# One head's exponential in every eighth forward unit moved from ScalarE to VectorE, its value product eight units later

## The chip, the cores and the metric

The kernel runs on one core of a Trainium2 chip (trn2). The metric is the device time of one execution in microseconds; the median of the runs is compared. The engines are TensorE (PE, with its weight loads as PEld), VectorE (DVE), ScalarE (ACT), GpSimd (POOL) and SyncE (SP, which only issues DMAs here).

## The reference, cut to what matters

One transformer block with adaptive layer norm, forward, and then the gradients of everything by its inputs and weights. One sequence of 2048 tokens, width 512, 32 heads of 16, a dense part of width 1792 with a squared ReLU. The change touches the attention of the forward pass only:

```python
h = _layernorm(x, axis=-1) * (1 + ca) + sa
qkv = (h @ wqkv).reshape(B, S, 3, H, Dh)          # H = 32, Dh = 16
scores = jnp.einsum('bhqd,bhkd->bhqk', q, k) * Dh ** (-0.5)
p = softmax(scores, axis=-1)
o = jnp.einsum('bhqk,bhkd->bhqd', p, v)
x = x + ga * (o.reshape(B, S, D) @ wo)            # then the dense part, then jax.vjp of it all
```

The softmax needs 32 x 2048 x 2048 exponentials in the forward pass; the backward pass computes them once more.

## The kernel before, in words

The program runs in four stages on one core: a short preparation, the forward pass with its attention (up to 996 us), the last quarter of the dense part, and then the attention's backward pass (from about 1100 us) with the gradients of the projections at the end. The instruction order of all engines is the order of the Python code (a manual schedule): each engine takes its own instructions strictly in that order.

**Forward units.** The attention is cut into 512 units: 4 query chunks of 512 tokens (`qc`), 8 head groups of 4 heads (`hg`), 16 key tiles of 128 tokens (`kt`, the innermost loop). In the loop over `u`, `fscore(u)` issues four score products on TensorE (L576: keys x queries, 128 x 512 per head). They go into two PSUM tiles `psST` of two banks each, one for each pair of heads; the pool holds three such tiles. ScalarE turns each tile into bfloat16 exponentials with one 128x1024 instruction (L578), into the unit's SBUF tile `ET`, of which there are four. Two units later `fpv(u)` multiplies the four heads' exponentials with the values (L592), in four 32-column strips of the array, and adds them into the one PSUM bank `oacc`. After the sixteenth key tile VectorE copies `oacc` out (`ostage`, L596); a row of ones in the values gives the softmax's denominator with it. The maximum is bounded beforehand and enters through an extra row of the queries, so that no maximum is taken over the scores. Two idle products of `steady` (L615) fill units that have no other product.

**Work fitted between.** The unit loop also carries everything else of the forward pass. A plan of tasks by unit number fills the first 100 units: the other heads' projections, norms, transposes. From unit 130 on, `dense_chunk` runs as a generator, one product per unit, over the dense part of the query chunk just finished (chunks 0, 1 and 2; the fourth comes after the forward units). Its parts are, in order: the attention output and its layer norm (L348 to L377), the first dense product with ReLU and square (L410, L412, L413), the dense gradient (L424, L427), four long sums each for the input gradient (L446) and the dense output (L500), and the attention gradient (L532). Between them `next_chain` issues weight gradients (L233) and VectorE copies each out (`part`, L251). All these products share a single PSUM bank (`mm()`, tag `pm`, a pool of one): a product can't begin before VectorE has emptied the bank of the one before it.

**Order on the engines.** A unit issues, in this order: what `later(lag, ...)` has put off to this unit (`run_due`), the scores and exponentials of unit u, the value products of unit u-2, the planned task or the dense step with its evictions. VectorE does the evictions and all elementwise work of the dense part; GpSimd sums rows (`racc`, L170), scales (`gf_c`, L307), copies `obf` (L604) and issues the loads of keys and queries.

Of the kernel before, what the change touches and what calls it, by code (L numbers as in the profile page):

```python
# [28 lines left out]
SCALE = 0.25  # L29
EPS = 1e-5  # L30
QPAD = 528


@with_exitstack
def kernel(
# [111 lines left out]
    with ExitStack() as ph:  # L147
# [32 lines left out]
        def later(lag, f, *args):  # L180
            due.append((unit[0] + lag, f, args))
# [371 lines left out]

        funits = [(qc, hg, kt) for qc in range(QC) for hg in range(HG) for kt in range(TT)]
        fh, fe, fcur, fdone, dense = {}, {}, {}, [], []

        def fload(qc, hg):
            i = hg % 2
# [8 lines left out]
        def fscore(u):  # L567
            qc, hg, kt = funits[u]
            qt_sb, kt_sb = fh[qc, hg]
            ET = ework.tile([P, 4, 512], BF, name="ET", tag="ET")  # L570
            fe[u] = ET
            for pair in range(2):
                ps = pools["s"].tile([P, 2, 512], F32, name="psST", tag="psST")
                for hi in range(2):
                    r = 32 * (2 * pair + hi)
                    PE.matmul(ps[:, hi, :], kt_sb[r:r + 32, kt * P:(kt + 1) * P], qt_sb[r:r + 32, :],  # L576
                              start=True, stop=True, tile_position=(r, 0))
                ACT.activation(ET[:, 2 * pair:2 * pair + 2, :], ps[:], AF.Exp, scale=SCALE)  # L578

        def fpv(u):  # L580
            qc, hg, kt = funits[u]
            if kt == 0:
                fcur["o"] = pools["o"].tile([P, 512], F32, name="oacc", tag="oacc")
                if hg == 0:
                    fcur["rr"] = ework.tile([H, 512], F32, name="rrows", tag="rrows", bufs=1)
                    fcur["ou"] = ework.tile([P, 4, HG, P], BF, name="O_un", tag="O_un", bufs=1)
            oacc = fcur["o"]
            ET = fe.pop(u)
            for hq in range(4):
                h = hg * 4 + hq  # L590
                lhsT = vaug[:, kt].rearrange("p h c -> p (h c)")[:, h * (DH + 1):h * (DH + 1) + 32]
                PE.matmul(oacc[32 * hq:32 * hq + 32, :], lhsT, ET[:, hq, :],  # L592
                          start=(kt == 0), stop=(kt == TT - 1), tile_position=(0, 32 * hq), skip_group_check=True)
            if kt == TT - 1:
                ostage = ework.tile([P, 512], F32, name="ostage", tag="ostage", bufs=1)
                DVE.tensor_copy(ostage[:], oacc[:])  # L596
                obf = ework.tile([P, 512], BF, name="obf", tag="obf", bufs=2)
                if u == NF - 1:
                    fcur["last"] = ostage
                    return  # L600
                if hg == HG - 1:
                    DVE.tensor_copy(obf[:], ostage[:])
                else:
                    POOL.tensor_copy(obf[:], ostage[:])  # L604
                for hq in range(4):
                    h = hg * 4 + hq
                    later(2, sp, fcur["rr"][h:h + 1, :], ostage[32 * hq + 16:32 * hq + 17, :])
                later(3, sp, fcur["ou"][:, :, hg, :], obf[:], True)
                if hg == HG - 1:
                    fdone.append((u + 7, qc, fcur["rr"], fcur["ou"]))  # L610
# [622 lines left out]
        def last_chunk(O_c, L, w1T, w2T):  # L1233
# [29 lines left out]
            for half in range(2):  # L1263
# [30 lines left out]
                for ic in range(DC):  # L1294
# [4 lines left out]
                    else:  # L1299
                        DVE.tensor_scalar(to, pt[:, :, ic, :], modcol[:, 4, ic:ic + 1], modcol[:, 3, ic:ic + 1],  # L1300
                                          ALU.mult, ALU.add)
            db2bf = wk.tile([1, D], BF, name="db2bf", tag="db2", bufs=1)
            later(4, DVE.tensor_tensor, db2bf[:], pd[0:1, :], gb_bc[0:1, :], ALU.mult)
            later(6, sp, out_7.rearrange("(o f) -> o f", o=1), db2bf[:])
            later(len(dwq) + 2, sp, h2_c.rearrange("p t (i d) -> p (t i) d", d=P), h2T.rearrange("p t i q -> p (t i q)"), True)
# [716 lines left out]
```

## Time and profile before

| what | value |
|---|---|
| time, median of 3 runs | 2491.31 us (2484.18, 2491.31, 2497.56) |
| profiled execution, span from first to last instruction | 2501.3 us; the page gives no other time of that execution |
| mean granted TensorE clock | 0.980 |
| busy over the span: PE, ACT, DVE, POOL | 2324.0, 2303.7, 1837.7, 488.0 us |
| forward units: first and last start of an exponential | 41.2 and 995.1 us |
| exponentials L578 | 1024 instructions, 941.9 us busy |
| backward exponentials L1600 | 2048 instructions of 128x512 |

A group line gives the code line, the engine, the operation, what it writes and reads with shapes, the count, the busy time and the mean duration of one, and then the engine's idle time just before. Durations of neighbouring instructions of one engine overlap somewhat, so the rate of a group is read from the distance of starts or ends, not from the mean duration.

### The profile page before, as it was taken

How to read it: one execution, taken by the hardware profiler on the slowest of the kernel's cores; microseconds unless marked ns; L12 is line 12 of the kernel's file. 1: busy time of each engine (PE TensorE's matmuls, PEld its weight loads, DVE VectorE, ACT ScalarE, POOL GpSimd, SP SyncE). 2: the span in 40 equal slices, each digit the busy share in tenths (PEclk: the TensorE clock that was granted, in tenths of full speed). 3: DMA queues.
4: the chain of work that ended last, by engine and by line, in shares of the span. 5: the costliest groups of instructions: out<-in, count | busy, mean ns of one | idle time of the engine just before them, and what ended most of it. 6: DMA issues, size and time to landing. Idle time of an engine off the chain costs nothing.

```text
span 2501.3 us, 49888 instructions
## 1 busy us (share of the span) xinstructions
PE 2324.0 (93%) x18948; PEld 783.4 (31%) x19036; DVE 1837.7 (73%) x2377; ACT 2303.7 (92%) x3560; POOL 488.0 (20%) x661
## 2 busy tenths in 40 slices
PE   8899899989998998999999999999999999999989
PEld 3232233223332333443223323233232323332344
DVE  6555354455435444579989999999999999999965
ACT  7999999999998999539999999999999999999944
POOL 2111223323533453110111101111011110110100
PEclk9999999999998999999999999999999999999999
DMA  4468463258546865979999999999999999999984
GB/s 146 130 167 176 144 150 97 88 166 142 98 95 142 151 131 110 256 200 196 201 192 206 199 198 202 196 204 203 205 205 198 205 202 199 200 198 214 201 253 133
DMA packets 1189503, 437.70 MB, mean 175 GB/s; under 512 B 1065867, under 2 KB 1160521, under 8 KB 1188878
## 3 DMA queue, kind: packets, MB, share of 16 engines
q1 hardware_dynamic: 1152414, 389.35, 79.0%
q0 software_dynamic: 19872, 27.09, 6.5%
q10 hardware_dynamic: 16976, 18.07, 2.9%
q8 instruction: 149, 2.44, 0.4%
q14 instruction: 92, 0.75, 0.1%
HBM read 98.30 MB, written 70.80 MB: 68 GB/s over the span
## 4 chain that ended last, share of the span: by engine, by line
ACT 40%; PE 38%; issue 8%; DVE 7%; DMA 3%; SPq 1%; ACTq 1%; POOL 0%; DVEq 0%; another core or an unknown queue 0%; POOLq 0%
ACT E_u L1600 24%; ACT ET L578 12%; PE dqacc L1681 4%; PE psST L576 3%; PE psS_A L1594 3%; PE accVK L1654 2%; PE pm L233 2%; ACT dsT L1760 2%; PE psS_B L1594 2%; PE pdh L1858 2%; PE oacc L592 2%; PE psS_C L1594 2%; PE pwq L1892 2%; PE pm L500 2%; PE pm L410 2%
## 5 line engine op out<-in xcount | busy, mean ns | idle before, releaser
L1616 DVE TENSOR_TENSOR dS_u<-psD_u,E_u 128x1024 bf16<-128x1024 f32 x1024 | 1185.9, 1218 | 77.1 <-PE psD_u L1614 30.2
L578 ACT ACTIVATE ET<-psST 128x1024 bf16<-128x1024 f32 x1024 | 941.9, 1242 | 16.6 <-PE psST L576 16.3
L1600 ACT ACTIVATE E_u<-psS_A 128x512 bf16<-128x512 f32 x768 | 509.9, 664 | 10.8 <-PE psS_C L1594 8.5
L1600 ACT ACTIVATE E_u<-psS_B 128x512 bf16<-128x512 f32 x768 | 503.2, 655 | 10.8 <-DMA dsT<-dS_u 2.7
L1614 PE MATMUL psD_u<-iv,ido 32*128 32x512 bf16 x2048 | 409.1, 388 | 1.5 <-DVE dS_u L1616 1.3
L576 PE MATMUL psST<-qt_sb,kt_sb 32*128 32x512 bf16 x2048 | 313.8, 386 | 48.0 <-ACT ET L578 41.0
L1600 ACT ACTIVATE E_u<-psS_C 128x512 bf16<-128x512 f32 x512 | 334.3, 653 | 3.1 <-PE psS_B L1594 1.1
L1594 PE MATMUL psS_B<-ik,iq 32*128 32x512 bf16 x768 | 296.1, 386 | 11.7 <-ACT E_u L1600 4.4
L1594 PE MATMUL psS_A<-ik,iq 32*128 32x512 bf16 x768 | 294.5, 383 | 11.0 <-DVE dwlast L237 1.0
L1699 POOL TENSOR_TENSOR dQacc<-dQacc,dqtmp 128x512 f32<-128x512 f32 x64 | 81.2, 1268 | 858.8 <-ACT dqtmp L1694 797.4
L1594 PEld LDWEIGHTS <-iq 32*128 32x128 bf16 x2048 | 129.7, 91 | 313.9 <-issue 296.9
L1654 PE MATMUL accVK<-dS_u,qz 128*32 128x512 bf16 x2048 | 213.5, 388 | 0.5 <-PE psD_u L1614 0.2
L592 PE MATMUL oacc<-ET,vaug 128*32 128x512 bf16 x2048 | 207.0, 394 | 3.9 <-DVE ostage L596 3.9
L1663 PE MATMUL accVK<-E_u,dOs_tok 128*16 128x512 bf16 x2048 | 204.5, 388 | 0.0
L1594 PE MATMUL psS_C<-ik,iq 32*128 32x512 bf16 x512 | 194.2, 379 | 4.5
L576 PEld LDWEIGHTS <-kt_sb 32*128 32x128 bf16 x2048 | 84.3, 91 | 328.2 <-issue 306.5
L1681 PE MATMUL dqacc<-dsT,KS_tok 128*32 128x512 bf16 x2048 | 145.7, 382 | 18.8 <-DMA dsT<-dS_u 5.0
L1760 ACT ACTIVATE dsT<-ptT 128x1024 bf16<-128x1024 bf16 x128 | 144.1, 1126 | 13.1 <-PE ptT L1644 12.2
L251 DVE COPY part<-pm 128x512 f32<-128x512 f32 (+2 forms) x106 | 65.2, 615 | 121.9 <-PE pm L233 111.8
L1614 PEld LDWEIGHTS <-ido 32*128 32x128 bf16 x2048 | 105.2, 91 | 101.3 <-issue 94.9
L1654 PEld LDWEIGHTS <-qz 128*32 128x32 bf16 x2048 | 58.5, 94 | 178.0 <-issue 162.9
L1699 POOL TENSOR_TENSOR dQst<-dQacc,dqtmp 128x512 bf16<-128x512 f32 x32 | 40.6, 1270 | 266.1 <-ACT dqtmp L1694 266.1
(415 smaller groups left out, 2688.7 us busy)
## 6 DMA issues: line engine op xcount, KB each, us to landing
p_st<-part POOLq DMA_DIRECT2D x36, 256.0 KB, 4.6
kt_sb<-qkT_st POOLq DMA_DIRECT2D x124, 64.0 KB, 3.0
wA<-in_B_w_dram SPq DMA_DIRECT2D x28, 256.0 KB
wB<-w1T_st SPq DMA_DIRECT2D x21, 256.0 KB
wA<-w2T_st SPq DMA_DIRECT2D x21, 256.0 KB
wB<-in_B_w_dram SPq DMA_DIRECT2D x21, 256.0 KB
p_st<-part POOLq DMA_DIRECT2D x28, 192.0 KB, 4.6
p_st<-part SPq DMA_DIRECT2D x18, 256.0 KB
```

Source lines behind the costliest of these rows:

```text
L576: PE.matmul(ps[:, hi, :], kt_sb[r:r + 32, kt * P:(kt + 1) * P], qt_sb[r:r + 32, :], start=True, stop=True, tile_position=(r, 0))
L578: ACT.activation(ET[:, 2 * pair:2 * pair + 2, :], ps[:], AF.Exp, scale=SCALE)
L592: PE.matmul(oacc[32 * hq:32 * hq + 32, :], lhsT, ET[:, hq, :], start=(kt == 0), stop=(kt == TT - 1), tile_position=(0, 32 * hq), skip_grou ...
L1594: PE.matmul(psS[:], st["q"][r:r + 32, qt * P:(qt + 1) * P], st["k"][r:r + 32, kc * 512:kc * 512 + 512], start=True, stop=True, tile_positi ...
L1600: ACT.activation(bst[u][0][:, hq, :], sst.pop((u, hq))[:], AF.Exp, scale=SCALE)
L1614: PE.matmul(psD[:, hi, :], st["do"][r:r + 32, qt * P:(qt + 1) * P], st["v"][r:r + 32, kc * 512:kc * 512 + 512], start=True, stop=True, til ...
L1616: DVE.tensor_tensor(dS_u[:, 2 * pair:2 * pair + 2, :], psD[:], E_u[:, 2 * pair:2 * pair + 2, :], ALU.mult)
L1654: PE.matmul(cur["vk"][32 * hq:32 * hq + 32, :], hst[hg]["qz"][:, qt, hq, :], bst[u][1][:, hq, :], start=(qt == 0), stop=False, tile_positi ...
L1663: PE.matmul(acc[32 * hq:32 * hq + DH, :], dOs_tok[:, qt, (hg * 4 + hq) * DH:(hg * 4 + hq + 1) * DH], E_u[:, hq, :], start=False, stop=(qt ...
L1681: PE.matmul(acc[32 * hq:32 * hq + 32, :], KS_tok[:, kc * 4 + kt, h * DH:h * DH + 32], tT[:, :, hq * 4 + kt, :], start=(kt == 0), stop=(kt ...
L1699: POOL.tensor_tensor(dst2, dst, tmp[:], ALU.add)
L1760: ACT.activation(dst, pt[:], AF.Identity)
```

## The change

In the units with `kt % 8 == 1` (64 of 512, two in each run of sixteen) the second pair's instruction on ScalarE covers only the third head (128x512). The fourth head goes to `vector_exp`: VectorE reads the score bank, multiplies by `SCALE*log2(e)` and clips, splits the exponent into an integer and a fraction by adding and subtracting a rounding constant, shifts the integer into the exponent bits, evaluates a polynomial of degree 4 of the fraction, and multiplies both into a bfloat16 result. These are nine instructions over 128x512, all but the last result in fp32: the first at once, the others one per unit over the next seven units, two of them in the third. The value product of that head is issued eight units after its scores, ahead of the four (or three) products of that moment, into the same `oacc`. It lies in the same head group: key tile 1's is issued with key tile 7, key tile 9's with key tile 15.

Three fp32 scratch tiles of 128x512 are added in SBUF; `ET` has three buffers instead of four, `obf` one instead of two, and a small tile of the last dense chunk takes its space from another ring.

```diff
+LOG2E = 1.4426950408889634
+ROUND = 12583039.0
+POW2 = (-0.6931241750717163, 0.24024099111557007, -0.055906426161527634, 0.009582852944731712)
...
-            ET = ework.tile([P, 4, 512], BF, name="ET", tag="ET")
+            ET = ework.tile([P, 4, 512], BF, name="ET", tag="ET", bufs=3)
...
-                ACT.activation(ET[:, 2 * pair:2 * pair + 2, :], ps[:], AF.Exp, scale=SCALE)
+                if pair == 1 and kt % 8 == 1:
+                    ACT.activation(ET[:, 2, :], ps[:, 0, :], AF.Exp, scale=SCALE)
+                    vector_exp(u, ps[:, 1, :])
+                else:
+                    ACT.activation(ET[:, 2 * pair:2 * pair + 2, :], ps[:], AF.Exp, scale=SCALE)
+
+        def vector_exp(u, s):
+            w, t, p = (ework.tile([P, 512], F32, name=f"vx{i}", tag=f"vx{i}", bufs=1) for i in range(3))
+            bits, res = t[:].bitcast(I32), p[:].bitcast(BF)[:, 0:512]
+            DVE.tensor_scalar(w[:], s, SCALE * LOG2E, -126.0, ALU.mult, ALU.max)
+            later(1, DVE.tensor_scalar, t[:], w[:], ROUND, None, ALU.add)
+            later(2, lambda: DVE.scalar_tensor_tensor(out=w[:], in0=t[:], scalar=ROUND, in1=w[:], op0=ALU.subtract, op1=ALU.subtract))
+            later(3, DVE.tensor_scalar, bits, bits, 23, None, ALU.logical_shift_left)
+            later(3, DVE.tensor_scalar, p[:], w[:], POW2[3], None, ALU.mult)
+            for lag, i, to in ((4, 2, p), (5, 1, p), (6, 0, w)):
+                later(lag, lambda i=i, to=to: DVE.scalar_tensor_tensor(out=to[:], in0=p[:], scalar=POW2[i], in1=w[:], op0=ALU.add, op1=ALU.mult))
+            later(7, lambda: DVE.scalar_tensor_tensor(out=res, in0=w[:], scalar=1.0, in1=t[:], op0=ALU.add, op1=ALU.mult))
+            flate[u + 8] = (u, res)
+
+        def value_product(u, hq, src):
+            h = funits[u][1] * 4 + hq
+            kt = funits[u][2]
+            lhsT = vaug[:, kt].rearrange("p h c -> p (h c)")[:, h * (DH + 1):h * (DH + 1) + 32]
+            PE.matmul(fcur["o"][32 * hq:32 * hq + 32, :], lhsT, src,
+                      start=(kt == 0), stop=(kt == TT - 1), tile_position=(0, 32 * hq), skip_group_check=True)
...
             ET = fe.pop(u)
+            if u + 2 in flate:
+                value_product(flate[u + 2][0], 3, flate.pop(u + 2)[1])
             for hq in range(4):
-                h = hg * 4 + hq
-                lhsT = vaug[:, kt].rearrange("p h c -> p (h c)")[:, h * (DH + 1):h * (DH + 1) + 32]
-                PE.matmul(oacc[32 * hq:32 * hq + 32, :], lhsT, ET[:, hq, :],
-                          start=(kt == 0), stop=(kt == TT - 1), tile_position=(0, 32 * hq), skip_group_check=True)
+                if hq < 3 or kt % 8 != 1:
+                    value_product(u, hq, ET[:, hq, :])
...
-                obf = ework.tile([P, 512], BF, name="obf", tag="obf", bufs=2)
+                obf = ework.tile([P, 512], BF, name="obf", tag="obf", bufs=1)
...
-            db2bf = wk.tile([1, D], BF, name="db2bf", tag="db2", bufs=1)
+            db2bf = wk.tile([P, D], BF, name="db2bf", tag="dxn2")[0:1, :]
```

More of the change, by code (lines that the diff above doesn't have):

```diff
@@ L555 @@
         fh, fe, fcur, fdone, dense = {}, {}, {}, [], []
+        flate = {}
         def fload(qc, hg):
```

## The prediction

> **What bounds the kernel now.** I read the page's slices first, then the exponentials' tile view, the windows by stage, and at last the timeline of single units.
>
> ```profile
> PE   8899899989998998999999999999999999999989
> DVE  6555354455435444579989999999999999999965
> ACT  7999999999998999539999999999999999999944
> ```
>
> The forward units fill the first sixteen slices. ScalarE is full there; VectorE is half free.
>
> ```profile
> L578 ACT ACTIVATE ET<-psST x1024: 1018/1206/1959, 41.2 to 995.1; 128x1024 bf16<-128x1024 f32 x171
>   PE psST L576: 16.3, 16
> ```
>
> From the first start to the last are 953.9 us, of which ScalarE waited 16.3. The rest is (953.9 - 16.3)/1023 = 0.917 us an exponential, 1.83 a unit. So the forward is ScalarE's, and time taken from ScalarE there counts if nothing else is nearly as slow. TensorE waits for ScalarE only in places; the next two views show what stands close behind.
>
> ```profile
> 566.65 0.57 PE L576 MATMUL psST<-qt_sb,kt_sb 32*128 32x512 bf16 x4
> 566.76 0.75 DVE L412 TENSOR_SCALAR rT<-pm,b1col 128x512 bf16<-128x512 f32 x1 [0.66 <-PE pm L410]
> 567.15 0.40 PE L592 MATMUL oacc<-ET,vaug 128*32 128x512 bf16 x4
> 567.55 0.42 DVE L413 TENSOR_TENSOR sT<-rT 128x512 bf16<-128x512 bf16 x1
> 567.57 1.02 PE L410 MATMUL pm<-h2T,wA 128*128 128x512 bf16 x4
> 568.52 0.53 PE L576 MATMUL psST<-qt_sb,kt_sb 32*128 32x512 bf16 x4
> ```
>
> This is one unit of the first dense product. The product starts 0.06 after the eviction before it ends (566.76 + 0.75), runs 1.02, and 0.04 to 0.1 later VectorE evicts again: a loop over the single bank, 568.52 - 566.65 = 1.87 us a unit, already longer than ScalarE's 1.83. A lead that TensorE brings along (three score tiles: 2 x 0.917 less about 0.5 for release and scores, 1.3 us) hides the difference over 14 units. VectorE has 0.66 free in each such unit.
>
> ```profile
> core 0: us, PE busy (x) PEld busy (x) DVE busy (x) ACT busy (x) POOL busy (x), PEclk, DMA share, GB/s
> 41.00:996.25 955.25, 860.24 (x5994) 283.25 (x6056) 473.11 (x933) 941.94 (x1024) 312.45 (x490) 0.99 0.58 132
> 187.00:201.00 14.00, 13.54 (x105) 4.45 (x102) 11.92 (x28) 14.00 (x17) 5.22 (x10) 1.00 0.58 121
> 331.00:345.00 14.00, 13.04 (x93) 4.77 (x93) 10.94 (x16) 14.00 (x17) 6.33 (x9) 1.00 0.51 125
> 604.00:643.00 39.00, 35.07 (x252) 12.41 (x256) 15.40 (x34) 39.00 (x43) 18.12 (x35) 1.00 0.91 125
> 780.00:799.00 19.00, 12.22 (x92) 4.48 (x90) 16.58 (x46) 14.63 (x16) 6.17 (x11) 0.85 0.38 95
> ```
>
> VectorE's 473 of 955 is no even half: 85% late in the planned tasks (187 us), 78% in L410's stage (331), 39% in the dense gradient (604), 87% in the third chunk's attention output (780), where ScalarE waits for it.
>
> **The change part by part.** *ScalarE* loses half an instruction in 64 units. Neighbouring 128x512 exponentials of the backward pass give its price:
>
> ```profile
> 1155.44 0.60 ACT L1600 ACTIVATE E_u<-psS_C 128x512 bf16<-128x512 f32 x1
> 1157.82 0.67 ACT L1600 ACTIVATE E_u<-psS_B 128x512 bf16<-128x512 f32 x1
> ```
>
> Five exponentials lie between their ends (1156.04 and 1158.49), 0.49 each. The saving is 64 x (0.917 - 0.49) = 27.3 us, and ScalarE's pace becomes 1.78 a unit, 14.24 for eight. Were a half call no cheaper than its recorded 0.60, it would be 20.
>
> *Loops that don't get shorter.* L410's loop stays at 1.87 and the alternation of L424 and L233 at 1.84 (sixteen units, whose first scores start at 600.38 and 629.83). Three chunks, each 14 units x 0.09 + 28 x 0.06 = 2.9, less the lead of 1.3 once: 4.8 are not gained.
>
> *VectorE* gains nine instructions in eight units. The first, from PSUM: 0.69 (L251, 128x512 fp32). The three with one SBUF source: 0.42 (L1034, 0.419 over 32 partitions; L602's cast takes 0.427 over 128). The five with two: 0.67 (L1035 to L1038, 0.671 to 0.674). Sum 0.69 + 1.26 + 3.35 = 5.3 us, 64 times 339 us; back to back, durations overlap by 0.07 each (L1034 starts at 121.69, the next at 122.02), so between 4.7 and 5.3. In all 473 + 339 = 812 of 928 us: it fits on average, and costs only where an eviction is late by it. By unit that is 0.34 to 0.84, queued ahead of the unit's eviction:
> - L424 and L233: 0.69 evicted of 1.84, 1.11 free (idle rows "1.11 <-PE pm L233"). Hidden; without that cover 0.66 a unit.
> - L410: 0.66 free against 0.67, and 0.84 in every eighth unit, which overruns by 0.15. Where `ostage` comes too (every sixteenth) the eviction is some 0.55 late. In four units of each chunk GpSimd's sum stretches `sT` from 0.42 to 1.23 and nothing is free. Bounds 0 and 7 us over three chunks; I take 4.
> - Third chunk's output, 780 to 799: VectorE alone sets the time. About seven units' insertions of 0.66 come in between: 4.5 (0 if they fell into its few gaps); I take 4.
> - The same part of chunks 0 and 1: half of its units have no product; bounds 0 and 4, I take 2.
> - Planned tasks around 187: 11.9 + 5.3 in a stretch of 14 is 3 too much, less 1.3 of lead: 2.
>
> Together 12. The first of the nine waits for the unit's second score pair; queued behind it are the unit's eviction and tasks, but their products come after those scores on TensorE as well, so that wait costs nothing by itself. The score tile comes free when both readers are done; VectorE's 0.69, if VectorE is free, ends before ScalarE's 0.49, which waits for the exponentials ahead of it.
>
> *TensorE* gets no product more. A fifth strip product in one unit of eight must wait for its strip: 0 (in the loops it falls into the wait for the eviction) to 0.25 (1.02/4). TensorE waits for ScalarE in most stretches, which hides it; 0.5 in all. It reads its operand one unit after VectorE's last step, so it waits only if VectorE is a whole unit late.
>
> *Edits at nothing.* Three `ET`: exponential u then needs the value products of u-3, which TensorE issued before the scores of u, for which the exponential waits anyway. One `obf`: it is written every 16 units (29 us) and read three units later. `db2bf`: its DMA goes out at the sixth tick, ring neighbours come after 28 products. No DMA is added or moved past another.
>
> Sum: 27.3 - 4.8 - 12 - 0.5 = 10. The span of 2501.3 lies 0.4% over the median; nothing around the span is listed, so I carry the 10 us to the median unscaled: 2491.3 - 10 = 2481.
>
> **The rivals.** *Full cover.* VectorE's queue absorbs nearly everything, since in 51 of 64 stretches of eight units TensorE, less its waits for ScalarE, needs under 14.24. Gain 27.3 - 4.8 = 23, 2468. For: 1.11 free in the commonest product units. Against: 87% at 780.
>
> *Given back.* L410's bounds at their upper end, and the planned tasks late at every product: 12 becomes 20; 2488. For: the loop has no slack of its own.
>
> *Slower: GpSimd holds VectorE.* GpSimd's elementwise work in the forward is about 117 us (L170, L307, L604, L429 groups), 12% of 955. During it VectorE's SBUF work stretches: `sT` took 0.42, and beside a row sum this:
>
> ```profile
> 339.16 2.44 POOL L170 TENSOR_TENSOR racc<-racc,g_c 128x512 f32<-128x512 f32 x2
> 339.35 1.23 DVE L413 TENSOR_TENSOR sT<-rT 128x512 bf16<-128x512 bf16 x1
> ```
>
> Eight of the nine new instructions are of that sort: 512 x 12% x 0.5 is 31 us more on VectorE, 5.8 per stretch of eight units. It decides once a stretch has over 14.24 - 5.8 = 8.4 us of own VectorE work. I cut the forward at every eighth unit and took VectorE's busy time in each: about 20 stretches are over it, by 45 us together. If that all reaches the path, the forward lasts 64 x 14.24 + 45 + 5 + 10 of stalls left = 971, 15 over its 955: 2506. Against: part of GpSimd's work lies where TensorE has slack. The Trainium skill (SBUF — State Buffer, "Who interferes with whom") states the rule beside it: a VectorE instruction with two SBUF inputs, or in a two-port mode, and a GpSimd instruction that reads SBUF exclude each other for a whole instruction. The stretched row agrees with it (1.23 for 0.42); by the rule the sum would move from a gain of 10 towards this loss of 15.
>
> *Not what it says.* A half call that starts no earlier would save nothing; the backward's 0.49 speaks against that: 2491 at best.
>
> **How the numbers follow.** Forecast 0.45, own range 2474 to 2488; full cover 0.24; given back 0.10; slower 0.18; not what it says 0.03. Half a per cent (12.5 us, about what a measurement can tell from no change) lies inside the forecast's own range: 0.16 of its 0.45 goes to faster. Faster 0.16 + 0.24 = 0.40, slower 0.17 (a hundredth of its rival stays within), same 0.43. The range runs from beyond full cover, 2466, to 2504, which leaves out the half of the slower rival that costs most.
>
> **What would show it.** Right: 960 exponentials of 128x1024 and 64 of 128x512 whose ends lie 0.49 apart; VectorE's forward busy near 800; L410 still at 1.87 with its idle gap gone; ScalarE's waits at 16.3 + 17 = 33; the last exponential some 10 us earlier. Wrong: ScalarE waits of 50 us, or new instructions of over 1 us beside GpSimd's sums, would mean the slower case; L410's units at 2 us or more, the one given back.

## The result and the profile after

The change makes the kernel slower: 2612.29 us (median of 4 runs, 2609.89 to 2614.36) against 2490.91 us for the kernel before on the same chip, a ratio of 1.0495 with a 95% interval of 1.0471 to 1.052. That is 121 us more, where 10 us less was forecast, and 108 us beyond the upper end of the range. The profiled execution lasts 2610.88 us with a span of 2609.1 and a mean granted clock of 0.964.

The last exponential starts 118 us later (1113.5 after, 995.1 before), so the loss lies in the forward. The slices of the page of after; the forward now fills seventeen of them:

```profile
PE   8788788887888688889999999999999999999989
DVE  6877686778686877657999999999999999999965
ACT  7998989887989787863999999999999999999954
PEclk9999999898999898999999999999999999999999
```

VectorE went up by two to three tenths in most forward slices, as it should. ScalarE, full in nearly every forward slice before, now has tenths missing in about half of them, and the granted clock reads eight tenths in four slices (in one before). The view of tile `ET` of after (minimum/median/maximum in ns, first and last start; below, what ScalarE waited for, in us and times):

```profile
L586 ACT ACTIVATE ET<-psST x960: 1017/1031/1368, 42.2 to 1113.5; 128x1024 bf16<-128x1024 f32 x192
L583 ACT ACTIVATE ET<-psST x64: 591/641/917, 45.0 to 1098.1; 128x512 bf16<-128x512 f32 x64
  PE psST L580: 143.2, 119
```

960 whole exponentials and 64 half ones are there, and in the trace the ends of a half one and of its predecessor lie 0.490 us apart (10th to 90th percentile 0.488 to 0.491), as priced. But ScalarE waits 143.2 us for scores, not 16.3. Taking work from ScalarE has made it wait for TensorE; the question is what TensorE waits for. The waits in the forward (engine, line, releaser; us in all, times, longest), of after:

```profile
DVE vx L591 <- ACT ET L583: 104.7, 47, 9.3
PE oacc L605 <- DVE ostage L624: 37.5, 27, 2.1
PE oacc L605 <- DVE vx L598: 22.3, 16, 4.5
```

The first line is new: the first of the nine instructions (L591) waits 47 times for *ScalarE's half exponential* (L583), 2.2 us each, though it reads another bank of the score tile. The second line was this in the kernel before (L592 and L596 are its L605 and L624):

```profile
PE oacc L592 <- DVE ostage L596: 3.9, 4, 1.2
```

The third line is new too, and is taken up further down. The unit with key tile 1 that starts near 106 us shows how the first two hang together (timeline of after: start, duration, engine, line, what; in brackets the idle time before it and its releaser):

```profile
106.18 0.60 PE L580 MATMUL psST<-qt_sb,kt_sb 32*128 32x512 bf16 x4
107.92 0.74 ACT L583 ACTIVATE ET<-psST 128x512 bf16<-128x512 f32 x1
108.70 0.69 DVE L591 TENSOR_SCALAR vx<-psST 128x512 f32<-128x512 f32 x1 [1.26 <-ACT ET L583]
109.31 0.68 DVE L624 COPY ostage<-oacc 128x512 f32<-128x512 f32 x1
109.90 0.68 DVE L1041 CAST sP<-pm 128x512 bf16<-128x512 f32 x1
110.04 0.40 PE L605 MATMUL oacc<-ET,vaug 128*32 128x512 bf16 x4 [1.42 <-DVE ostage L624]
111.44 3.06 ACT L586 ACTIVATE ET<-psST 128x1024 bf16<-128x1024 f32 x3 [0.79 <-PE psST L580]
```

The scores are there at 106.78. VectorE stands until ScalarE, which first works off the exponentials ahead, has done its half (108.66). Behind L591 in VectorE's queue wait the copy that frees the accumulator (L624) and the eviction of the dense product (L1041). The next head group's first value product needs the accumulator, so TensorE stands 1.42 us, the following scores come late, and ScalarE has nothing to do for 0.79. The two instructions read disjoint halves of one tile, and ScalarE's comes first in the program: the second reader waits for the first.

### The profile page after: what moved, and what is told of

Its sections match the earlier page's. It is cut to its first block, busy times and chain, and to the rows that moved or that the text cites. A ratio compares the mean times of both kernels' runs of the same rounds, so it can differ in the third digit from the quotient of the medians.

```text
span 2609.1 us, 50510 instructions
## 1 busy us (share of the span) xinstructions
PE 2336.4 (90%) x18950; PEld 782.8 (30%) x19036; DVE 2165.1 (83%) x2953; ACT 2290.3 (88%) x3560; POOL 503.8 (19%) x661
## 4 chain that ended last, share of the span: by engine, by line
ACT 37%; PE 35%; DVE 15%; issue 8%; DMA 3%; ACTq 1%; POOL 0%; DVEq 0%; SPq 0%; another core or an unknown queue 0%; POOLq 0%
ACT E_u L1628 23%; ACT ET L586 9%; PE dqacc L1709 4%; PE psS_A L1622 3%; PE accVK L1682 2%; ACT dsT L1788 2%; PE psS_B L1622 2%; PE psST L580 2%; PE psS_C L1622 2%; PE accVK L1691 2%; PE pdh L1886 2%; PE pm L236 2%; PE pwq L1920 2%; DVE vx L597 1%; PE oacc L605 1%
## 5 line engine op out<-in xcount | busy, mean ns | idle before, releaser
L586 ACT ACTIVATE ET<-psST 128x1024 bf16<-128x1024 f32 x960 | 902.1, 1061 | 146.4 <-PE psST L580 143.2
L580 PE MATMUL psST<-qt_sb,kt_sb 32*128 32x512 bf16 x2048 | 282.6, 401 | 34.1 <-ACT ET L586 25.7
L605 PE MATMUL oacc<-ET,vaug 128*32 128x512 bf16 x1984 | 228.7, 409 | 37.6 <-DVE ostage L624 37.5
L580 PEld LDWEIGHTS <-kt_sb 32*128 32x128 bf16 x2048 | 73.2, 91 | 302.1 <-issue 290.3
L597 DVE SCALAR_TENSOR_TENSOR vx<-vx,vx 128x512 f32<-128x512 f32 x192 | 147.6, 769 | 1.4
L591 DVE TENSOR_SCALAR vx<-psST 128x512 f32<-128x512 f32 x64 | 44.0, 688 | 104.9 <-ACT ET L583 104.7
L605 PEld LDWEIGHTS <-vaug 128*32 128x32 bf16 x2048 | 57.3, 94 | 184.6 <-issue 184.5
```

Source lines behind the costliest of these rows:

```text
L597: later(lag, lambda i=i, to=to: DVE.scalar_tensor_tensor(out=to[:], in0=p[:], scalar=POW2[i], in1=w[:], op0=ALU.add, op1=ALU.mult))
L605: PE.matmul(fcur["o"][32 * hq:32 * hq + 32, :], lhsT, src, start=(kt == 0), stop=(kt == TT - 1), tile_position=(0, 32 * hq), skip_group_ch ...
```

## The experiments

All times below are differences to the kernel before, run on the same chip beside each kernel.

**Where the wait comes from: the order of the two readers.** The two lines are swapped, so that ScalarE's half waits for VectorE instead.

```diff
-                    ACT.activation(ET[:, 2, :], ps[:, 0, :], AF.Exp, scale=SCALE)
                     vector_exp(u, ps[:, 1, :])
+                    ACT.activation(ET[:, 2, :], ps[:, 0, :], AF.Exp, scale=SCALE)
```

> The same instructions as in the changed kernel, but VectorE's read of the fourth head's score bank is issued ahead of ScalarE's 128x512 exponential of the third head, so VectorE waits for TensorE alone and ScalarE waits for VectorE's read of the same tile instead. Theory A (the held queue: in the changed kernel VectorE's first instruction waits until ScalarE has finished the other half of the same score tile, 104.7 us in 47 of 64, and the evictions of the one product bank queue up behind it): most of the loss goes, 2475 to 2510 us; ScalarE's waits for scores fall from 143 us to below 60. Theory B (the work itself: 379 us more on VectorE, stretched beside GpSimd's sums, makes evictions late): the loss stays, 2590 to 2630 us, since no VectorE instruction is taken away.

Measured: 2566.89 against 2487.81, ratio 1.0314 [1.0285, 1.0343]: 79 us over before, 42 less than the change. That lies between the two theories: the held queue is a part of the loss, and not most of it. L591 no longer waits for ScalarE but for TensorE's scores, 41.7 us in 20 places; TensorE's wait for the copy falls from 37.5 to 9.5 us. And ScalarE now waits for L591, 44.0 us in 24 places. The longest of these, in the timeline of this kernel:

```profile
299.40 5.81 POOL L310 TENSOR_TENSOR gf_c<-g_c,modbc 128x512 bf16<-128x512 bf16 x4 [14.21 <-DMA g_c<-in_grad_out_dram]
299.49 6.27 DVE L647 TENSOR_TENSOR O_c<-O_un,r_inv 128x512 bf16<-128x512 bf16 x4
305.69 0.68 DVE L591 TENSOR_SCALAR vx<-psST 128x512 f32<-128x512 f32 x1
306.40 0.60 ACT L584 ACTIVATE ET<-psST 128x512 bf16<-128x512 f32 x1 [5.82 <-DVE vx L591]
307.05 0.61 PE L580 MATMUL psST<-qt_sb,kt_sb 32*128 32x512 bf16 x2 [5.28 <-ACT ET L584]
```

Four scalings of VectorE last 6.27 us beside four of GpSimd; the score tile waits for VectorE behind them, and with it ScalarE (5.82) and TensorE (5.28). So the reader of a score tile brings its whole queue onto the ring of three score tiles, whichever of the two goes first.

**The fourth head in a score tile of its own.** No instruction now shares a tile with another engine; the ring of three gives a third tile in those units.

```diff
+                    to = ps[:, hi, :]
+                    if 2 * pair + hi == 3 and kt % 8 == 1:
+                        own = pools["s"].tile([P, 2, 512], F32, name="psOwn", tag="psST")
+                        to = own[:, 0, :]
...
-                    vector_exp(u, ps[:, 1, :])
+                    vector_exp(u, own[:, 0, :])
```

> As the changed kernel, but in the 64 units the fourth head's scores go into a score tile of their own (a third one of the ring of three), so that neither reader waits for the other; the price is a shorter lead of TensorE in those units. Theory A: 2475 to 2515 us, VectorE's first instruction waits for TensorE only. Theory B: 2590 to 2630 us.

Measured: 2593.76, ratio 1.0419 [1.0388, 1.045], 106 us over before. The time fits theory B, but a part of it is new waits. The wait between the readers is gone, and TensorE's wait for the copy falls to 8.0 us. But VectorE's instruction now stands for TensorE's scores, as the prediction had it, and holds up its queue there (its waits in the forward):

```profile
DVE vx L595 <- PE psOwn L584: 65.9, 38, 9.7
```

The third tile of the ring is used up besides: TensorE waits 26.2 us for ScalarE to free one for the fourth head, and ScalarE's waits for scores stay at 124.2 us (after: 143.2). As a remedy it is worse than the swap.

**What is saved on ScalarE, by itself.** The half exponential alone; the fourth head's exponential and value product are left out in the 64 units.

```diff
-                    vector_exp(u, ps[:, 1, :])
```

> Leaves out the fourth head's exponential in the 64 units and its value product: ScalarE's half is saved, VectorE gets nothing. Both theories: the gross gain without VectorE, 23 us by the prediction's sum (27.3 less 4.8 in the loops), so 2463 to 2472 us; less than 15 us of gain would mean that the loops over the product bank hold more of the forward than was reckoned.

Measured: 2478.72, ratio 0.9975 [0.995, 1.0]: 9 us less, where 23 were expected. In its trace the span from the first to the last end of an exponential is 937.6 us (954.0 in the trace of before), 16.5 us less; each is one execution. So the most that the change could have earned, with VectorE's part for nothing, is some 9 to 16 us.

**The wait by itself.** The kernel before with one VectorE instruction on the second bank behind the whole exponential, its result unused, and three buffers of `ET`.

```diff
                 ACT.activation(ET[:, 2 * pair:2 * pair + 2, :], ps[:], AF.Exp, scale=SCALE)
+                if pair == 1 and kt % 8 == 1:
+                    w = ework.tile([P, 512], F32, name="vx0", tag="vx0", bufs=1)
+                    DVE.tensor_scalar(w[:], ps[:, 1, :], SCALE, -126.0, ALU.mult, ALU.max)
```

> The kernel before with its whole exponentials, and in the 64 units one VectorE instruction (128x512, PSUM to SBUF, 0.69 us, result unused) that reads the second score tile after ScalarE's exponential of it and so waits for ScalarE; nothing else of the change but the three ET buffers. Theory A: the wait alone costs, 40 to 110 us more than before (2530 to 2600 us), with VectorE waiting for ScalarE some 80 to 110 us in all. Theory B: 64 x 0.69 = 44 us of VectorE work that mostly fits, 0 to 10 us more.

Measured: 2594.39, ratio 1.0425 [1.0401, 1.0448], 107 us over before, as theory A had it, for 64 instructions of 0.69 us whose results nobody reads. Its waits in the forward (L581 is the added instruction, L599 the copy to `ostage`, L595 the value product):

```profile
DVE vx L581 <- ACT ET L578: 184.6, 57, 15.3
PE oacc L595 <- DVE ostage L599: 55.7, 31, 1.9
```

and one such unit in its timeline:

```profile
501.77 0.60 PE L576 MATMUL psST<-qt_sb,kt_sb 32*128 32x512 bf16 x4
502.88 0.69 DVE L581 TENSOR_SCALAR vx<-psST 128x512 f32<-128x512 f32 x1 [4.84 <-ACT ET L578]
503.49 0.68 DVE L599 COPY ostage<-oacc 128x512 f32<-128x512 f32 x1
504.09 0.68 DVE L251 COPY part<-pm 128x512 f32<-128x512 f32 x1
504.23 0.40 PE L595 MATMUL oacc<-ET,vaug 128*32 128x512 bf16 x4 [1.85 <-DVE ostage L599]
506.48 1.94 ACT L578 ACTIVATE ET<-psST 128x1024 bf16<-128x1024 f32 x2 [1.79 <-PE psST L576]
506.87 1.57 PE L233 MATMUL pm<-a_c,O_c 128*128 128x512 bf16 x4
```

VectorE stands idle for 4.84 us, its copy goes out at 503.49, TensorE stands 1.85 us for it, and ScalarE stands 1.79. The last line is a second price: the four products of a step, 1.04 us elsewhere, take 1.57, because the granted clock is halved there (its record: 3.413 us at 0.5 from 504.6 on).

**The same instruction one unit later, and only in one of the two units.** First `later(1, DVE.tensor_scalar, ...)` in place of the direct call, behind the unit's eviction and the copy of the accumulator:

```diff
-                    DVE.tensor_scalar(w[:], ps[:, 1, :], SCALE, -126.0, ALU.mult, ALU.max)
+                    later(1, DVE.tensor_scalar, w[:], ps[:, 1, :], SCALE, -126.0, ALU.mult, ALU.max)
```

> Control to the kernel with one waiting VectorE instruction and whole exponentials (2594 us): the same instruction with the same wait for ScalarE, issued one unit later, behind the eviction and the copy of oacc. Theory A (what queues up behind the wait costs, not the instruction): within 15 us of before, 2480 to 2503 us. If the instruction or its hold on the score tile costs by itself: 2530 us or more.

Measured: 2503.53, ratio 1.0056 [1.0035, 1.0076], 16 us over before instead of 107. The work is the same, so 91 us came from where the instruction stands. It still waits for ScalarE, though less (L188 is the line that issues it here):

```profile
DVE vx L188 <- ACT ET L578: 56.3, 26, 14.0
```

But the copy is now ahead of it, and TensorE waits 3.9 us for the copy, as in the kernel before.

Then at once, as at first, but in key tile 9 alone (32 units), where no copy of the accumulator is queued behind it:

```diff
-                if pair == 1 and kt % 8 == 1:
+                if pair == 1 and kt == 9:
```

> The kernel with one waiting VectorE instruction, but only in the 32 units with kt = 9; the 32 with kt = 1, in which VectorE's copy of oacc stands directly behind the waiting instruction, are left as before. If each wait costs alike: half of the 105 us, 2535 to 2545 us. If the copy of oacc behind it is what stops TensorE (27 of that kernel's 36 half-clock periods begin two or three units after kt = 1): a quarter or less, 2488 to 2515 us.

Measured: 2515.15, ratio 1.0111 [1.0083, 1.0138], 28 us, about a quarter. VectorE still waits 95.5 us for ScalarE there, but TensorE waits only 3.9 us for the copy. By difference the 32 units with key tile 1 cost 107 - 28 = 79 us, 2.5 each: what makes the wait dear is the copy behind it.

**The load by itself.** The nine instructions run on a constant in SBUF, on the same schedule; ScalarE and the value products are as before. Their results are not used.

```diff
+            if kt % 8 == 1:
+                vector_exp(u, identf.unsqueeze(1).to_broadcast([P, 4, P]))
```

> The kernel before with its whole exponentials, and beside them the nine VectorE instructions of the change, in the same places, working on a constant in SBUF; their result is not used. VectorE's load without any tie to the score tiles and without the late value product. Theory A (VectorE's new waits and its queue reaching the score tiles make the loss): 0 to 25 us more than before, 2488 to 2513 us. Theory B (the load itself makes evictions late): 80 us more or beyond, 2570 us and up, as in the kernel in which neither reader waits for the other (2594 us).

Measured: 2547.92, ratio 1.0239 [1.02, 1.0279], 60 us, without any new wait on a score tile. That is between the two theories; the prediction had 12. One of its two largest items, of 4 us each, was the product loop of L410, which is line L413 in this kernel. Timeline of the load alone, in that loop (L415 evicts, L595 is one of the nine):

```profile
347.64 0.75 DVE L415 TENSOR_SCALAR rT<-pm,b1col 128x512 bf16<-128x512 f32 x1
348.43 0.43 DVE L416 TENSOR_TENSOR sT<-rT 128x512 bf16<-128x512 bf16 x1
348.77 0.69 DVE L595 SCALAR_TENSOR_TENSOR vx<-vx,vx 128x512 f32<-128x512 f32 x1
349.51 0.75 DVE L415 TENSOR_SCALAR rT<-pm,b1col 128x512 bf16<-128x512 f32 x1
```

The loop turns at 349.51 - 347.64 = 1.87, with its gap filled, just as forecast, and so do ten of the thirteen distances between its evictions in each chunk. The other three are 2.06, 3.38 and 2.75 (1.94, 1.85 and 1.87 in the kernel before): the copy `ostage` and GpSimd's row sums come there. The same loop, 8 us later:

```profile
356.03 2.45 POOL L173 TENSOR_TENSOR racc<-racc,g_c 128x512 f32<-128x512 f32 x2
356.08 1.38 DVE L416 TENSOR_TENSOR sT<-rT 128x512 bf16<-128x512 bf16 x1
357.39 1.38 DVE L191 TENSOR_SCALAR vx<-vx 128x512 f32<-128x512 f32 x1
359.48 1.02 PE L413 MATMUL pm<-h2T,wA 128*128 128x512 bf16 x4 [1.69 <-DVE rT L415]
```

Beside the two sums `sT` (0.43 above) and one of the nine (0.42 elsewhere) take 1.38 each, and TensorE stands 1.69 us for the eviction behind them.

More is lost ahead of the loop, where VectorE prepares its input. The same kernel, some ten us before the loop's first lines above:

```profile
335.99 1.41 DVE L595 SCALAR_TENSOR_TENSOR vx<-vx,vx 128x512 f32<-128x512 f32 x2
337.44 0.69 DVE L596 SCALAR_TENSOR_TENSOR vx<-vx,vx 128x512 bf16<-128x512 f32 x1
338.05 1.36 DVE L380 TENSOR_SCALAR h2T<-ptC,modcol 128x256 bf16<-128x256 bf16 x4
339.46 1.03 PE L351 MATMUL ptC<-identb,xn_c 128*128 128x128 bf16 x8 [2.49 <-DVE h2T L380]
341.14 8.35 ACT L582 ACTIVATE ET<-psST 128x1024 bf16<-128x1024 f32 x9 [2.67 <-PE psST L580]
```

and the same place in the kernel before (L377 and L348 are its L380 and L351):

```profile
321.84 1.36 DVE L377 TENSOR_SCALAR h2T<-ptC,modcol 128x256 bf16<-128x256 bf16 x4
323.26 0.62 PE L348 MATMUL ptC<-identb,xn_c 128*128 128x128 bf16 x8 [0.53 <-DVE h2T L377]
```

The scalings of `h2T` follow their transposes at once before; now three of the nine instructions, which had piled up, go first and take 338.05 - 335.99 = 2.06 us; TensorE stands 2.49 us instead of 0.53 and ScalarE 2.67. Cut at every eighth unit by the ends of the exponentials, the trace of the load alone loses 62 us against that of the kernel before. The last column is from the next two kernels, which leave out GpSimd's row sums:

| place (units) | predicted, us | load alone against before | both without the sums |
|---|---|---|---|
| planned tasks (80 to 104) | 2 | 6.5 | 3.5 |
| output and norm of chunks 0 and 1 (144 to 160, 272 to 288) | 2 | 11.2 | 7.6 |
| third chunk's output (392 to 408) | 4 | 7.6 | 9.7 |
| loop of L410 (160 to 176, 288 to 304, 408 to 432) | 4 | 7.6 | 1.3 |
| L424 and L233 (176 to 208, 304 to 328) | 0 | 0.1 | 0.1 |
| long sums of L446 (208 to 232, 328 to 360, 456 to 488) | not listed | 16.9 | 0.0 |
| all else in the forward | not listed | 12 | 12 |

At the third chunk's output the kernel without the sums and without the load is itself 4.8 us faster than the kernel before, hence the 9.7.

**How much of the load is GpSimd's hold on VectorE.** GpSimd's row sums are left out, once with the load and once in the kernel before; only the first term of each sum remains.

```diff
-                    POOL.tensor_tensor(racc[:, j, :], racc[:, j, :], src, ALU.add)
```

> The kernel with VectorE's load only (2548 us), without GpSimd's adding of row sums (L173; the sums are left out but for the first tile). To be read against the kernel before without those sums. Theory G (GpSimd's elementwise work holding VectorE is what makes the load late): no more than 35 us over its control. Theory Q (VectorE's queue in its full stretches, with or without GpSimd): 50 us or more over its control.

> Control: the kernel before without GpSimd's adding of row sums (left out but for the first tile). Both theories: 2478 to 2492 us, since in the kernel before ScalarE sets the time in the forward and GpSimd is off the path.

Measured: 2525.31 with the load (ratio 1.0154 [1.0134, 1.0174], 36 us over before), 2488.13 without it (1.0 [0.9984, 1.0015]). So the load costs 37 us without the sums, a little over theory G's bound, and 60 with them: 23 us of it come from the sums beside it (give or take 12, by the intervals), which by themselves cost nothing. By the table above these us lie in the loop of L410 and in the long sums of L446, where without GpSimd's sums next to nothing is lost. The group of the three polynomial steps, first in the load alone (by line and form: count, busy us and mean ns of one, idle before):

```profile
L595 DVE SCALAR_TENSOR_TENSOR vx<-vx,vx 128x512 f32<-128x512 f32 x192 | 146.2, 761 | 1.4
```

and without the sums:

```profile
L593 DVE SCALAR_TENSOR_TENSOR vx<-vx,vx 128x512 f32<-128x512 f32 x192 | 136.1, 709 | 1.4
```

The mean falls from 761 to 709 ns, against a median of 684 and 682. In the trace of the load alone seventeen of the instructions with two sources last 1.63 to 1.65 us, each beside a sum of 1.2 to 1.4 us, like this one (its timeline):

```profile
449.52 1.19 POOL L173 TENSOR_TENSOR racc<-racc,prod 128x512 f32<-128x512 f32 x1
449.62 1.64 DVE L591 SCALAR_TENSOR_TENSOR vx<-vx,vx 128x512 f32<-128x512 f32 x1
```

Without the sums there is none of that length; one of 5.4 us, beside the four scalings `gf_c`, is in both.

**The change without the wait, and without the late product.** The first instruction goes one unit later (the change otherwise whole); then, besides, the late value product is left out.

```diff
-            DVE.tensor_scalar(w[:], s, SCALE * LOG2E, -126.0, ALU.mult, ALU.max)
+            later(1, DVE.tensor_scalar, w[:], s, SCALE * LOG2E, -126.0, ALU.mult, ALU.max)
```

> As the changed kernel, but VectorE's first instruction is put off by one unit, so that the unit's eviction and the copy of oacc go ahead of it and ScalarE has nearly finished the other half of the tile when VectorE comes to it. Theory A: the wait for ScalarE falls from 104.7 us to below 30, and the time lies under that of the kernel with the two readers swapped, 2495 to 2545 us. Theory B: 2570 to 2615 us.

```diff
             if u + 2 in flate:
-                value_product(flate[u + 2][0], 3, flate.pop(u + 2)[1])
+                flate.pop(u + 2)
```

> As the kernel with VectorE's first instruction one unit later (2558 us), but without the late value products (the fourth head's part of 64 units is left out of the sums). If TensorE's wait for VectorE's last step matters (22.5 us in 16 places, with half-clock stretches behind them): 2525 to 2545 us. If it is only a place where a stall shows that would come anyway: 2552 to 2560 us.

Measured: 2558.15, ratio 1.028 [1.0247, 1.0313], 71 us over before, and 2549.01, ratio 1.0252 [1.0229, 1.0276], 60 us. Both lie between their theories. L591's wait for ScalarE falls from 104.7 us to 30.4 in the first, and TensorE's for the copy from 37.5 to 6.0. The late product costs some 11 us, with an uncertainty of 10.

**Only where VectorE is free.** The swapped order, in twelve units behind which the swapped kernel took less time than the kernel before.

```diff
+ONVEC = (1, 33, 57, 65, 73, 105, 113, 121, 129, 201, 257, 385)
...
-                if pair == 1 and kt % 8 == 1:
+                if pair == 1 and u in ONVEC:
```

> The change in only 12 of the 64 units, with VectorE's read ahead of ScalarE's half: units 1, 33, 57, 65, 73, 105, 113, 121, 129, 201, 257 and 385, behind each of which the kernel with the two readers swapped took 14.2 to 14.4 us for eight units instead of the 14.67 of before. If the losses are where VectorE has no room, and nowhere else: 12 x 0.43 = 5 us under before, 2480 to 2486 us. If the losses move to other places: at or above before.

Measured: 2487.14 against 2489.16, ratio 0.9996 [0.9979, 1.0013]: no difference that shows. Twelve times 0.43 us of ScalarE are 5 us at most, and the interval, which reaches to 5 us less, neither shows them nor rules them out. No complete version here beats the kernel before; the half exponential alone leaves work out.

**Keeping TensorE busy in its pause.** The wait alone costs far more than the 55.7 us for which TensorE stands for the copy. To see whether the half clock behind such pauses makes up the difference, the second score pair of key tile 2 is computed five times over (the same values into the same tile), which fills about 0.85 us of the pause: in the kernel before as a price of the filling, in the wait alone, and in the change.

```diff
-                for hi in range(2):
+                for hi in [0, 1] * (5 if pair == 1 and kt == 2 else 1):
```

> The kernel before with the second score pair of every unit kt = 2 computed five times over (the same values into the same tile; 32 units, eight matmuls more, some 0.85 us each). It is the price of the filling alone. Both theories: TensorE has slack there, 0 to +12 us (0.995 to 1.005).

> The wait alone (one VectorE instruction behind ScalarE's exponential) with the same filling: TensorE computes 0.85 us in the place where it stood 1.85 us for the copy of oacc, 31 times, so that its pause shrinks to about 1 us; VectorE is as late as before. Theory A (the half clock after the pause makes most of the loss): few half-clock periods are left (under 12, was 36) and the loss falls from 106 to 40 to 55 us, by the 0.66 us that a stretch of eight units without half clock lost in the wait alone (2530 to 2545). Theory B (VectorE's lateness itself costs it): the loss stays at 95 to 120 us (2585 to 2610), whatever the clock.

> The whole change with the same filling. Theory A: 27 half-clock periods become 15 or fewer, ratio 1.02 to 1.035 (2540 to 2575), since the product's waits for the copy (37.5 us of TensorE's waits) are the ones filled and those for the late product and the score ring remain. Theory B: 1.045 to 1.055, as without the filling.

| kernel | us over before | ratio | half-clock periods in the forward, us in all |
|---|---|---|---|
| before | 0 | | 5, 24 |
| before, filled | 14 | 1.0061 [1.0037, 1.0084] | 7, 31 |
| wait alone | 107 | 1.0425 [1.0401, 1.0448] | 36, 154 |
| wait alone, filled | 88 | 1.0353 [1.0323, 1.0384] | 22, 99 |
| change | 121 | 1.0495 [1.0471, 1.052] | 27, 126 |
| change, filled | 124 | 1.0497 [1.0473, 1.0521] | 24, 113 |

In the wait alone the filling halves TensorE's pause:

```profile
PE oacc L595 <- DVE ostage L599: 28.9, 31, 1.0
```

14 half-clock periods go, and with them 18 us (give or take 10, by the intervals), or 32 if the filling's own price of 14 (12 at most was expected) is added back: 1.3 to 2.3 us a period. By that estimate the 31 periods that the wait adds to before's five are 40 to 71 of its 107 us; the upper figure is too high, since products take at most about twice as long at half clock (1.89 us for 1.04, further down), so that 154 - 24 = 130 us of it can take some 65 from TensorE. TensorE's longer standing for the copy (55.7 less 3.9, 52 us) and 40 to 65 for the clock make 92 to 117, if both reach the path in full: together they can account for the 107. The expectation for the wait alone was missed: 22 periods remain where theory A had under 12, and 88 us lie between its 40 to 55 and theory B's 95 to 120. In the whole change the filling bought nothing, as theory B had it: 24 periods of 27 are left, though the waits for the copy fell from 37.5 to 14.5 us. There the pauses have other causes besides the copy: in the wait alone a half-clock period begins within 3.5 us of 25 of the 31 waits for the copy, in the change of 9 of the 27. No run has the wait with the full clock throughout, so the exact share of the clock stays open.

## Why the prediction was wrong

The terms, each by difference of the runs to their kernels before; they add up to the measured 121 because each is the step from one run to the next. Each step is uncertain by some 10 us, and in another order the sizes would differ (the wait alone costs 107, but 51 once VectorE is late anyway):

| term | predicted | measured | from |
|---|---|---|---|
| saved on ScalarE, less the loops | -22.5 | -9 | half exponential alone |
| VectorE's load | +12 | +60 | load alone; 23 of it with GpSimd's sums |
| tie to the score tile, late product | +0.5 | +19 | change one unit later, less the two above; the product 11 |
| wait of the first instruction | 0 | +51 | change, less change one unit later |
| sum | -10 | +121 | |

*The step that failed first* is the sentence "The first of the nine waits for the unit's second score pair ... so that wait costs nothing by itself". It named TensorE as the releaser. The releaser is ScalarE, because both readers take one tile and program order ties them, and ScalarE first works off what is queued ahead, 1.88 us from the scores' end to its own in the unit shown. The prediction listed what is queued behind that instruction, as one must, and then excused it with the wrong releaser. The same error sits in "VectorE's 0.69, if VectorE is free, ends before ScalarE's 0.49": in the timeline of after it starts 0.04 us after ScalarE's end, and the tile comes free 0.7 us later than without it. Whether the wait would have been free with TensorE as the releaser, no run shows by itself: with the swap and with a tile of its own VectorE does wait for scores, 41.7 and 65.9 us, and both kernels stay over the load alone (79 and 106 us against 60), but other waits have a part in that. No rival had this mechanism; the slower rival's 2506 came from the load alone.

*VectorE's load* is a mis-sized term, 12 for 60. L424 and L233 hide theirs, as forecast. L410's loop stays at 1.87 with its gap filled except where `ostage` and GpSimd's sums come; the prediction named just these units, bounded them by 7 and took 4, and they cost 7.6. In the change itself nine of the thirteen distances between evictions of that loop (358 to 388 us) are 1.85 to 1.87, and four are 2.5 to 3.5. Too small were the stretches between the loops, where VectorE's work is a chain that TensorE waits for step by step (normalisation, `h2T`, the planned tasks, the scalings of `O_c`): 2 + 2 + 4 for 25 us. And the long sums of L446, 17 us, were at nothing: the prediction's list has no item for them. VectorE's forward busy, forecast "near 800", shows that an average can be right while its use is wrong. Windows of after:

```profile
41.00:1115.00 1074.00, 877.51 (x6000) 284.77 (x6064) 802.24 (x1513) 929.78 (x1025) 328.52 (x490) 0.94 0.52 118
```

802 us as forecast, and the last exponential is 118 us late. The nine instructions' groups sum to 379, not 339 (records of neighbours overlap, so that sums of groups run above the union in this view).

*GpSimd's hold on VectorE* was the named mechanism of the slower rival and is there: 23 us by the runs with and without the sums. The rival priced it at 31 us more of VectorE's time; in the load alone the sums lengthen the nine instructions by 25 us (360 for 335 in all). The Trainium skill (SBUF — State Buffer, "Who interferes with whom") has it that a VectorE instruction with two inputs in SBUF and a GpSimd instruction that reads SBUF exclude each other for whole instructions; the seventeen of 1.64 us, 0.96 over the median beside sums of 1.2 to 1.4, agree. GpSimd's hold was given a chance of 0.18 as a rival by itself; it should have been a term of the forecast.

*ScalarE's saving* was right per piece (0.490 apart, 0.914 in the median otherwise) and was put at 22.5 in all, of which the trace of the half exponential alone shows 16.5 and its time 9 (0 to 12). ScalarE's waits for scores rise from 16.3 to 22.8 us there, so TensorE sets the pace in more places than assumed.

*TensorE's 0.5* for the late product rested on "it waits only if VectorE is a whole unit late". It is, 16 times: the waits above show 22.3 us for L598. In the swapped kernel one of them reads:

```profile
478.43 0.69 DVE L598 SCALAR_TENSOR_TENSOR vx<-vx,vx 128x512 bf16<-128x512 f32 x1
479.18 0.50 PE L605 MATMUL oacc<-vx,vaug 128*32 128x512 bf16 x1 [1.52 <-DVE vx L598]
480.03 1.89 PE L236 MATMUL pm<-a_c,O_c 128*128 128x512 bf16 x4
```

TensorE stands 1.52 us for the last of the nine and then runs its next four products at half clock (1.89 for 1.04).

Of the signs named for "right", the 960 and 64 exponentials and VectorE's 800 us came, which fit the slow kernel as well; ScalarE's waits of 33 us did not. Of the signs named for "wrong", ScalarE's waits passed 50 us by far. New instructions over 1 us are the exception, 32 of 576; these signs pointed to the slower rival, and its 15 us are an eighth of the loss.

## What to carry to other kernels

Before a second engine is given part of a tile, ask which instruction the program puts ahead of it on that tile and how far that engine lags; whatever is queued behind the new reader inherits the lag, and here 64 instructions of 0.69 us cost 107 us so and 16 us one unit later. VectorE, half idle on average, had that idle time in some loops and little of it in the stretches between them, so a load is to be priced stretch by stretch through the whole forward, above all where the engine's work alternates with TensorE's or meets GpSimd's. Measure first what the saving alone is worth: here 9 us, which left next to nothing to spend on the other engine.

## What was not expected of the hardware

The granted clock falls to half well before TensorE is idle. In the records the half-clock periods of the forward last 3.413 us or a multiple, and in each trace all begin on one grid of 3.413 us. Six traces (before, change, wait alone, load alone, and wait and change with the filling), cut into these windows from 60 to 1110 us, give 1654 windows at full clock. How many were followed by a window at half clock, by the share of the window in which a matmul ran:

| share of TensorE's time | windows | followed by half clock |
|---|---|---|
| under 0.50 | 75 | 65 |
| 0.50 to 0.65 | 116 | 49 |
| 0.65 to 0.80 | 263 | 18 |
| over 0.80 | 1200 | 0 |

The Trainium skill (TensorE: Matmul & The Clock Gate, "Part 1: The HAM clock gate (the "warmup" mystery)") states the free-running window of 3413 ns, and the records agree; it gives the half rate to a window of idle, and here windows with 0.50 to 0.65 of their time in matmuls were followed by it 49 times in 116. A single pause of 1.5 to 2 us in a forward whose TensorE is otherwise 90% busy (860 of 955 us) was often enough: in the wait alone, whose 31 waits for the copy last 1.8 us on average, half clock followed 25 of them. By the estimate from the filling such a period costs 1.3 to 2.3 us beyond the pause.
